# The head of a fused state-space and feed-forward kernel: tile 1 in two loads, weights ahead of tiles 2 and 3, all layernorm sums on VectorE, more of the first copies on ScalarE

## The chip, the cores and the metric

The kernel runs on one core of a Trainium2 chip. The metric is the device time of one execution in microseconds (us); lower is better. A profile records one execution; its span (first to last instruction) is mostly about 1.4 us shorter than the time that goes with it. All executions quoted here were in the fast state with a granted clock of 1.00.

## The reference

```python
xn = layernorm(x)                        # x: 2048 x 1024, bf16
A = 2 * real(C h) + xn * Dskip           # h[t] = Lam_bar * h[t-1] + B_bar xn[t], complex, 1024 states
B = (mish(x @ w1 + b1)) @ w2             # w1: 1024 x 3584, w2: 3584 x 1024, x here is xn
out = x + A + B
```

Both branches take the layernormed rows. They are worked in four blocks of 512 rows, each of four tiles of 128 rows. Everything that follows is about the first block's start, "the head": four tiles have to be loaded, normalised and transposed before the long run of matmuls can begin at full width.

## The kernel before

Each engine has its own program, a queue of operations in fixed order, with semaphore waits worked out from reads and writes. An operation that waits holds up all that stands behind it on its engine (in after_short below, VectorE stands 1.39 us at one tile's sums, and another tile's apply waits behind them). All loads of the head are issued by SyncE in this order: tile 0 in two halves, tile 1, tile 3, weight load 1, tile 2, weight loads 2 to 6, the skip weights, weight load 7. (The code's `ring` items are counted from 1 here; each is 512 KB.)

```python
    for h in range(2):
        SP.dma(lambda e, h=h: e.dma_start(xx[:, 0, 0, h * 512:(h + 1) * 512], A_x[0, 0:P, h * 512:(h + 1) * 512]),
               DmaSem(nc, "d_x00_%d" % h), writes=[b_xx[0][0].parts[h]])
    for q in (1, 3):
        load_x(SP, 0, q)
    # ... cut: small parameter loads ...
    for i in range(NRING):
        ring_load()
        if i == 0:
            load_x(SP, 0, 2)
        if i == 5:
            SP.dma(...)                      # skip weights, 256 KB
```

Tiles 0 to 2 get mean and variance on VectorE (`first_sums_v` twice, `first_var_v`), tile 3 gets them on ScalarE (two passes with accumulation). The root is taken on ScalarE; reciprocal and `first_apply` (subtract mean, multiply) are on VectorE. PE transposes the normalised tile, and `first_copy` brings it from PSUM to `xnT`. Fillers, matmuls on zeros, are meant to keep PE's clock up while it waits.

```python
    def keep_busy(n, behind=()):             # n fillers, all into PSUM bank 3
        for i in range(n):
            PE.mm(...)                       # 128 x 128; the first waits for `behind` and for bank 3

    keep_busy(36)
    for q in range(2):
        first_sums_v(q, 0); first_sums_v(q, 1); first_var_v(q); first_sqrt(q)
    keep_busy(14, [b_mv[0]])
    PE.op(...)                               # transpose of the parameters
    keep_busy(8, [b_mv[1]])
    first_apply(0)
    first_transpose(0)
    first_apply(1, 2)
    first_transpose(1)
    keep_busy(8)
    first_mean_a(3)                          # tile 3 on ScalarE
    first_copy(0, VE, 0, 4); first_copy(1, VE, 0, 4)
    first_copy(0, AC, 4, NK); first_copy(1, AC, 4, NK)
    first_center_a(3)
    # ... cut: parameters out of PSUM ...
    for h in range(2):
        first_sums_v(2, h)
    first_var_v(2)
    first_var_a(3)
    first_sqrt(2); first_sqrt(3)
    first_apply(2); first_apply(3)
    NSPLIT = 5
```

The first weight columns f are multiplied in two halves. The first half (tiles 0 and 1, 256 columns wide) can start while tiles 2 and 3 are still on their way; the second half follows in the main loop. Each `first_half(f, 0)` is eight matmuls over k. Weight loads 1 and 2 hold the lower and upper k of f = 0 to 3, loads 3 and 4 those of f = 4 to 7.

```python
    for f in range(4):
        first_half(f, 0, 0, NK // 2)         # load 1
    for f in range(4):
        first_half(f, 0, NK // 2, NK)        # load 2
        if f in (2, 3):
            first_transpose(f)
            first_copy(f, VE)
    first_half(4, 0)                         # loads 3 and 4
    # main loop: first_half(f, 1) for f < NSPLIT, then whole columns from f = NSPLIT on
```

Of the kernel before, what the change touches and what calls it, by code (L numbers as in the profile page):

```python
# [5 lines left out]
ALU = mybir.AluOpType  # L6
AF = mybir.ActivationFunctionType
DT = mybir.dt

P = 128  # L10
# [146 lines left out]
def build_kernel(nc, A_x, A_Lambda_re, A_Lambda_im, A_B_re, A_B_im, A_C_re, A_C_im,  # L157
                 A_log_dt, A_Dskip, B_w1, B_b1, B_w2, out):
    bf16, f32, i32 = DT.bfloat16, DT.float32, DT.int32
    S, D = A_x.shape[1], A_x.shape[2]  # L160
# [15 lines left out]
    VE = Queue(nc, "ve")  # L176
    AC = Queue(nc, "ac")
    PO = Queue(nc, "po")
    SP = Queue(nc, "sp")

    def sb(name, shape, dtype):
        return nc.alloc_sbuf_tensor(name, shape, dtype)
# [25 lines left out]
    xx = sb("xx", [P, 2, NQ, D], bf16)  # L208
    b_xx = [[Buf("xx%d_%d" % (i, q), parts=[Buf("xx%d_%d_%d" % (i, q, h)) for h in range(2)])
             for q in range(NQ)] for i in range(2)]  # L210
# [16 lines left out]
    mv = sb("mv", [P, NQ, 2], f32)  # L227
    b_mv = [Buf("mv%d" % i) for i in range(NQ)]
    rs = sb("rs", [P, NQ, 4], f32)
    b_rs, b_rs1 = ([Buf("rs%s%d" % (n, i)) for i in range(NQ)] for n in "ab")  # L230
    kon = sb("kon", [P, 3], f32)
    b_kon = Buf("kon")
# [9 lines left out]
    def c(n):  # L242
        return cs[:, CN.index(n), :]
# [7 lines left out]
    def ps16(i):  # L251
        return ps[:, i, :].bitcast(bf16)
# [6 lines left out]
    def scratch(name, where, i, dtype, n):  # L259
        if where == "h":  # L260
            t = nc.alloc_sbuf_tensor_at(name, [P, n], dtype, offset=base_h + 2048 * i)
            return t, Buf(name, parts=flat_hT[2 * i:2 * i + 2])
        t = nc.alloc_sbuf_tensor_at(name, [P, n], dtype, offset=base_a + 2048 * i)
        return t, Buf(name, parts=b_actf[2 * i:2 * i + 2])
# [11 lines left out]
    vop, aop, pop = VE.op, AC.op, PO.op  # L276
# [7 lines left out]
    def load_x(queue, blk, q):  # L284
        r0 = blk * TB + q * P
        i = blk % 2
        queue.dma(lambda e: e.dma_start(xx[:, i, q, :], A_x[0, r0:r0 + P, :]),  # L287
                  s_xx[i][q] if blk else s_x0[q], writes=[b_xx[i][q]])

    for h in range(2):  # L290
        SP.dma(lambda e, h=h: e.dma_start(xx[:, 0, 0, h * 512:(h + 1) * 512], A_x[0, 0:P, h * 512:(h + 1) * 512]),
               DmaSem(nc, "d_x00_%d" % h), writes=[b_xx[0][0].parts[h]])
    for q in (1, 3):
        load_x(SP, 0, q)
    for src, r0, n in ((A_log_dt, 2 * NJ, NJ), (A_Lambda_im, NJ, NJ), (A_Lambda_re, 0, NJ),
                       (B_b1, 3 * NJ, NF)):
        AC.dma(lambda e, src=src, r0=r0, n=n: e.dma_start(
# [24 lines left out]

    for i in range(NRING):
        ring_load()
        if i == 0:
            load_x(SP, 0, 2)
        if i == 5:
            SP.dma(lambda e: e.dma_start(dsk[:], A_Dskip.partition_broadcast(P)), s_dsk, writes=[b_dsk])

# [11 lines left out]



    sq, b_sq = scratch("sq", "a", 13, bf16, D)

    def rc(q, n):
        return rs[:, q, n:n + 1]

    def first_sums_v(q, h):
        s = q % 2  # L350
        vop(lambda e: e.bn_stats(stats[:, s, h, :], xx[:, 0, q, h * 512:(h + 1) * 512]),  # L351
            reads=[b_xx[0][q].parts[h]], writes=[b_stats[s]])

    def first_var_v(q):
        s = q % 2
        vop(lambda e: e.bn_aggr(mv[:, q, :], stats[:, s, :, :]), reads=[b_stats[s]], writes=[b_mv[q]])  # L356

    def first_mean_a(q):
        aop(lambda e: e.activation(sq[:], xx[:, 0, q, :], AF.Identity, bias=kon[:, 1:2], accum_out=rc(q, 3)),
            reads=[b_xx[0][q], b_kon], writes=[b_sq, b_rs[q]])  # L360

    def first_center_a(q):
        aop(lambda e: e.activation(mv[:, q, 0:1], rc(q, 3), AF.Copy, scale=-1.0 / D),
            reads=[b_rs[q]], writes=[b_mv[q]])

    def first_var_a(q):
        aop(lambda e: e.activation(sq[:], xx[:, 0, q, :], AF.Square, bias=mv[:, q, 0:1], accum_out=mv[:, q, 1:2]),
            reads=[b_xx[0][q], b_mv[q]], writes=[b_sq, b_mv[q]])

    def first_sqrt(q):  # L370
        scale = 1.0 if q < 3 else 1.0 / D
        aop(lambda e: e.activation(rc(q, 1), mv[:, q, 1:2], AF.Sqrt, scale=scale, bias=kon[:, 2:3]),
            reads=[b_mv[q], b_kon], writes=[b_rs1[q]])

    def first_apply(q, pieces=1):
        y = rc(q, 1)
        vop(lambda e: e.reciprocal(y, y), reads=[b_rs1[q]], writes=[b_rs1[q]])  # L377
        for h in range(pieces):
            d = slice(h * D // pieces, (h + 1) * D // pieces)
            b_x, b_o = (b_xx[0][q], b_xn[q]) if pieces == 1 else (b_xx[0][q].parts[h], b_xn[q].parts[h])  # L380
            vop(lambda e, d=d: e.tensor_scalar(xn[:, q, d], xx[:, 0, q, d], mv[:, q, 0:1], y,
                                               op0=ALU.subtract if q < 3 else ALU.add, op1=ALU.mult),
                reads=[b_x, b_mv[q], b_rs1[q]], writes=[b_o])

    def bank_T(q, k):
        if q < 2 and k >= NK // 2:
            return 4 + q
        return 6 + q % 2

    def first_transpose(q):  # L390
        for k in range(NK):
            bank = bank_T(q, k)
            PE.mm(lambda e, k=k, bank=bank: e.transpose(ps16(bank)[:, k * P:(k + 1) * P],  # L393
                                                        xn[:, q, k * P:(k + 1) * P], ident[:]),
                  reads=[b_xn[q].parts[k // (NK // 2)], b_ident], writes=[b_ps[bank]],
                  first=k == 0 or bank != bank_T(q, k - 1), last=k == NK - 1 or bank != bank_T(q, k + 1))

    def first_copy(q, queue, k0=0, k1=NK):
        dst = xnT[:, k0:k1, q * P:(q + 1) * P]
        bank = bank_T(q, k0)  # L400
        srcp = ps16(bank).rearrange("p (k t) -> p k t", k=NK)[:, k0:k1, :]
        b_dst = b_xnT[q] if k1 - k0 == NK else b_xnT[q].parts[k0 // 4]
        if queue is AC:
            aop(lambda e: e.copy(dst, srcp), reads=[b_ps[bank]], writes=[b_dst])
        else:
            vop(lambda e: e.tensor_copy(dst, srcp), reads=[b_ps[bank]], writes=[b_dst])
# [68 lines left out]
    def keep_busy(n, behind=()):  # L475
        for i in range(n):
            PE.mm(lambda e: e.matmul(ps[:, 3, 0:P], lhsT=filler[:], rhs=filler[:], start=True, stop=True),  # L477
                  reads=[b_filler] + (list(behind) if i == 0 else []), writes=[b_ps[3]], first=i == 0, last=i == n - 1)

    keep_busy(36)  # L480
    aop(lambda e: e.activation(rs[:, :, 3], kon[:, 2:3].to_broadcast([P, NQ]), AF.Sqrt), reads=[b_kon], writes=b_rs)
    for q in range(2):
        first_sums_v(q, 0)
        first_sums_v(q, 1)
        first_var_v(q)
        first_sqrt(q)
    keep_busy(14, [b_mv[0]])
    PE.op(lambda e: e.transpose(ps16(2)[:, 0:NST], st[:, :], ident[0:NST, 0:NST]),
          reads=[b_st, b_ident], writes=[b_ps[2]])
    keep_busy(8, [b_mv[1]])  # L490
    first_apply(0)
    first_transpose(0)
    first_apply(1, 2)
    first_transpose(1)
    keep_busy(8)
    first_mean_a(3)
    first_copy(0, VE, 0, 4)
    first_copy(1, VE, 0, 4)
    first_copy(0, AC, 4, NK)
    first_copy(1, AC, 4, NK)  # L500
    first_center_a(3)
    vop(lambda e: e.tensor_copy(par[:, :], ps16(2)[:, 0:NST]), reads=[b_ps[2]], writes=[b_par])
    for h in range(2):
        first_sums_v(2, h)
    first_var_v(2)
    first_var_a(3)
    first_sqrt(2)
    first_sqrt(3)
    first_apply(2)
    first_apply(3)  # L510
    NSPLIT = 5

    def w1_tile(base, f, k):

# [4 lines left out]
    def first_half(f, half, k0=0, k1=NK):  # L519
        ts = slice(half * 256, half * 256 + 256)  # L520
        for k in range(k0, k1):
            s, w = w1_tile(0, f, k)
            PE.mm(lambda e, k=k, w=w: e.matmul(ps[:, f, ts], lhsT=w, rhs=xnT[:, k, ts],  # L523
                                               start=k == 0, stop=k == NK - 1),
                  reads=[b_ring[s]] + [b.parts[k // 4] for b in b_xnT[2 * half:2 * half + 2]], writes=[b_ps[f]],
                  first=half == 0 and k == 0, last=half == 1 and k == NK - 1)
# [2 lines left out]
        first_half(f, 0, 0, NK // 2)  # L529
    for f in range(4):  # L530
        first_half(f, 0, NK // 2, NK)
        if f in (2, 3):
            first_transpose(f)
            first_copy(f, VE)
    first_half(4, 0)
    aop(lambda e: e.activation(c("dt"), ldt, AF.Exp), reads=[b_par], writes=[b_cs["dt"]])
    small("a", "dt", lre, ALU.mult)
    small("th", "dt", lim, ALU.mult)
# [120 lines left out]
    def first_tile(blk, f):  # L659
        bank, hs = f % 8, f % (2 * GF)  # L660
        if blk == 0 and f < NSPLIT:
            first_half(f, 1)
        for k in range(0 if blk == 0 and f < NSPLIT else NK):
            s, w = w1_tile(n_item[0], f % 4, k)
# [236 lines left out]
```

## Time and profile before

| | before |
|---|---|
| median time | 621.53 us (3 executions), 621.50 us (6) |
| span of the profile | 620.0 us |
| PE busy | 616.7 us, 99% |
| first real matmul | 8.70 us |
| second halves begin | 14.17 us |

The page of the kernel before: span, busy time by engine, the clock granted in 40 slices (tenths), and one of the costliest groups (busy us and mean ns, then idle time ahead of it).

```profile
span 620.0 us, 7386 instructions
...
PE 616.7 (99%) x2961; PEld 287.2 (46%) x2961; DVE 462.4 (75%) x677; ACT 247.6 (40%) x161; POOL 50.6 (8%) x47
...
PEclk9999999999999999999999999999999999999999
...
L665 PE MATMUL ps<-xnT,ring 128*128 128x512 bf16 x856 | 185.4, 379 | 0.0
```

PE is busy 99% of the time, and this group, like PE's other great ones, has 0.0 us of idle time ahead of it. Busy PE time is not a measure of how near PE is to its peak, but the missing waits say that only the head can be shortened by rearranging.

The timeline of PE's weight loads (PEld) of the kernel before shows the head's order. Its columns are start, length, engine, line, operation, output and inputs, forms, count, and in brackets the idle time before and what ended it. PEld is used because all weight loads have records, while some matmul records are missing in the traces (the changed kernel's page counts 2981 loads and 2925 matmuls). "xn" marks transposes, "xnT,ring" real matmuls.

```profile
7.13 1.07 PEld L393 LDWEIGHTS ps<-ident,xn 128*128 128x128 bf16 x16 [0.16 <-DVE xn L381]
8.16 0.49 PEld L477 LDWEIGHTS ps<-filler 128*128 128x128 bf16 x8
8.70 1.66 PEld L523 LDWEIGHTS ps<-xnT,ring 128*128 128x128 bf16 x16
10.57 1.21 PEld L523 LDWEIGHTS ps<-xnT,ring 128*128 128x128 bf16 x12 [0.21 <-DMA ring<-in_B_w_dram]
11.88 0.46 PEld L393 LDWEIGHTS ps<-ident,xn 128*128 128x128 bf16 x8
12.29 0.37 PEld L523 LDWEIGHTS ps<-xnT,ring 128*128 128x128 bf16 x4
12.67 0.54 PEld L393 LDWEIGHTS ps<-ident,xn 128*128 128x128 bf16 x8
13.17 0.81 PEld L523 LDWEIGHTS ps<-xnT,ring 128*128 128x128 bf16 x8
14.17 4.26 PEld L523 LDWEIGHTS ps<-xnT,ring 128*128 128x128 bf16 x40 [0.19 <-DVE xnT L406]
```

Fillers and the transposes' first wait (0.16 us) last until 7.13 us. Sixteen transposes and eight more fillers follow, and the first real matmul comes at 8.70. After it there are three holes worth naming: 0.21 us for weight load 2, 0.10 us ahead of tile 2's transposes (11.78 to 11.88), and 0.19 us for tile 3's copy. The second halves begin at 14.17.

The timeline of VectorE (DVE) of the kernel before, in the same columns:

```profile
9.05 1.42 DVE L351 BATCH_NORM_STATS2 stats<-xx 128x6 f32<-128x512 bf16 x2 [0.34 <-DMA xx<-in_A_x_dram]
...
11.28 0.55 DVE L381 TENSOR_SCALAR xn<-xx,mv,rs 128x1024 bf16<-128x1024 bf16 x1
11.74 0.16 DVE L377 RECIPROCAL rs<-rs 128x1 f32<-128x1 f32 x1
12.00 0.55 DVE L381 TENSOR_SCALAR xn<-xx,mv,rs 128x1024 bf16<-128x1024 bf16 x1
12.54 0.69 DVE L406 COPY xnT<-ps 128x1024 bf16<-128x1024 bf16 x1
13.43 0.69 DVE L406 COPY xnT<-ps 128x1024 bf16<-128x1024 bf16 x1 [0.19 <-PE ps L393]
```

VectorE waits 0.34 us for tile 2's load, then does tile 2's sums, and applies tile 2 (11.28) and tile 3 (12.00) one after the other. Nothing of tile 3's sums stands between them.

Landings are not in these lines. I read them from the trace as the end of a load's last transfer: in this profile tile 1 at 4.78 us, tile 3 at 5.92, weight load 1 at 7.59, tile 2 at 9.02, load 2 at 10.53, load 3 at 12.04, load 4 at 13.54.

### The profile page before, as it was taken

To read this page: it belongs to the slowest core of one execution; us is meant where nothing else is said; L and a number is where in the kernel's file an instruction comes from. 1 tells how busy PE (TensorE), PEld (TensorE's weight loads), DVE (VectorE), ACT (ScalarE), POOL (GpSimd) and SP (SyncE) were. 2 spreads that over 40 slices of the span, in tenths; PEclk is the share of its full clock that TensorE was granted. 3 is DMA by queue.
4 is the path that set the end of the run, shared out by engine and by line. 5 is a ranking of instruction groups with operands and counts; after the bars stand their busy time and mean duration, and the time that the engine had idled before them with its cause. 6 is when DMAs were issued, how large, how long until landed. Compare 5 with 4: busy or idle time off the path is not lost.

```text
span 620.0 us, 7386 instructions
## 1 busy us (share of the span) xinstructions
PE 616.7 (99%) x2961; PEld 287.2 (46%) x2961; DVE 462.4 (75%) x677; ACT 247.6 (40%) x161; POOL 50.6 (8%) x47
## 2 busy tenths in 40 slices
PE   9999999999999999999999999999999999999998
PEld 7544444444444444444444444444444444444444
DVE  7897999999467599998147659999624856999603
ACT  5689996440079940000008992000001999000000
POOL 1998000000100000000010000000000000000000
PEclk9999999999999999999999999999999999999999
DMA  8999956840364301783054430276203542033001
GB/s 282 255 294 248 220 111 190 218 136 0 124 204 147 135 1 36 205 197 107 17 187 135 150 122 1 85 204 174 82 35 104 169 167 69 1 122 117 1 0 69
DMA packets 95804, 79.41 MB, mean 128 GB/s; under 512 B 48922, under 2 KB 78234, under 8 KB 95770
## 3 DMA queue, kind: packets, MB, share of 16 engines
q1 hardware_dynamic: 92272, 71.64, 42.1%
q10 hardware_dynamic: 2538, 4.14, 1.8%
q0 software_dynamic: 960, 3.15, 1.6%
q8 instruction: 24, 0.39, 0.3%
q14 instruction: 10, 0.08, 0.0%
HBM read 63.19 MB, written 4.19 MB: 109 GB/s over the span
## 4 chain that ended last, share of the span: by engine, by line
PE 99%; DVE 1%; DMA 0%; issue 0%; DVEq 0%
PE ps L744 49%; PE ps L665 30%; PE ps L686 18%; PE ps L523 1%; DVE stats L351 0%; DMA xx<-in_A_x_dram 0%; PE ps L393 0%; PE ps L758 0%; PE ps L477 0%; DVE xx L812 0%; DVE mv L356 0%; DVE rs L377 0%; DVEq L131 0%
## 5 line engine op out<-in xcount | busy, mean ns | idle before, releaser
L744 PE MATMUL ps<-ring,act 128*128 128x512 bf16 x896 | 194.0, 379 | 0.0
L665 PE MATMUL ps<-xnT,ring 128*128 128x512 bf16 x856 | 185.4, 379 | 0.0
L644 ACT ACTIVATE act<-hb 128x3584 bf16<-128x3584 bf16 x16 | 50.9, 3183 | 224.1 <-DVE hb L673 224.0
L744 PEld LDWEIGHTS ps<-ring,act 128*128 128x128 bf16 x896 | 87.7, 98 | 105.7
L665 PEld LDWEIGHTS ps<-xnT,ring 128*128 128x128 bf16 x856 | 83.7, 98 | 100.8
L673 DVE TENSOR_SCALAR hb<-ps,par 128x512 bf16<-128x512 f32 x112 | 82.4, 747 | 56.0 <-PE ps L665 54.8
L686 PE MATMUL ps<-xnT,BT 128*128 128x512 bf16 x512 | 111.2, 379 | 0.0
L744 PE MATMUL ps<-CT,hT 128*128 128x512 bf16 x506 | 109.9, 379 | 0.0
L691 DVE TENSOR_TENSOR mt<-ps,tab 128x1024 bf16<-128x1024 f32 x64 | 75.4, 1219 | 17.5 <-PE ps L686 16.6
L686 PEld LDWEIGHTS ps<-xnT,BT 128*128 128x128 bf16 x512 | 50.1, 98 | 60.4
L744 PEld LDWEIGHTS ps<-CT,hT 128*128 128x128 bf16 x506 | 49.5, 98 | 59.7
L709 DVE TENSOR_TENSOR_SCAN hT<-cs,qi,hT 128x512 bf16<-128x512 f32 x48 | 58.9, 1269 | 0.0
L789 DVE TENSOR_TENSOR xx<-ps,xx 128x1024 bf16<-128x1024 f32 (+1 forms) x16 | 18.8, 1190 | 46.0 <-PE ps L744 45.9
L645 ACT ACTIVATE act<-act 128x3584 bf16<-128x3584 bf16 x16 | 51.0, 3190 | 0.2
L646 ACT ACTIVATE act<-act 128x3584 bf16<-128x3584 bf16 x16 | 51.0, 3190 | 0.2
L714 DVE TENSOR_TENSOR mt<-hT,tab 128x1024 bf16<-128x1024 bf16 x64 | 41.4, 688 | 1.1
L651 DVE TENSOR_TENSOR act<-act,hb 128x3584 bf16<-128x3584 bf16 x16 | 32.3, 2017 | 1.3 <-ACT act L646 1.3
L287 POOL DMA_DIRECT2D xx<-in_A_x_dram x12 | 6.7, 559 | 253.2 <-DVE xx L789 247.9
L620 ACT ACTIVATE ct<-CT,cs 128x512 f32<-128x512 bf16 x16 | 11.5, 720 | 26.7 <-DVE CT L622 25.9
L645 ACT ACT_TABLE_LOAD x16 | 20.5, 1283 | 0.3
L646 ACT ACT_TABLE_LOAD x16 | 20.5, 1283 | 0.3
L709 DVE TENSOR_TENSOR_SCAN hT<-cs,hT 128x512 bf16<-128x512 f32 x16 | 18.7, 1209 | 0.0
(86 smaller groups left out, 276.7 us busy)
## 6 DMA issues: line engine op xcount, KB each, us to landing
ring<-in_B_w_dram SPq DMA_DIRECT2D x112, 512.0 KB, 4.1
out_dram<-xx ACTq DMA_DIRECT2D x15, 256.0 KB, 2.1
xx<-in_A_x_dram POOLq DMA_DIRECT2D x12, 256.0 KB, 3.5
xx<-in_A_x_dram SPq DMA_DIRECT2D x3, 256.0 KB, 3.7
xx<-in_A_x_dram SPq DMA_DIRECT2D x2, 128.0 KB, 2.2
dsk<-in_A_Dskip_dram SPq DMA_DIRECT2D x1, 256.0 KB, 8.2
xnT<-xn SPq DMA_TRANSPOSE x12, 4.6
BT<-in_A_B_re_dram SPq DMA_TRANSPOSE x8, 6.2
```

The costliest lines, as they stand in the source:

```text
L644: aop(lambda e: e.activation(a, hs, AF.Exp), reads=[b_hb[g % 2]], writes=[b_act[g]])
L645: aop(lambda e: e.activation(a, a, AF.Ln, bias=1.0), reads=[b_act[g]], writes=[b_act[g]])
L646: aop(lambda e: e.activation(a, a, AF.Tanh), reads=[b_act[g]], writes=[b_act[g]])
L651: vop(lambda e: e.tensor_tensor(a, a, hs, op=ALU.mult), reads=[b_act[g], b_hb[g % 2]], writes=[b_act[g]])
L665: PE.mm(lambda e, k=k, w=w: e.matmul(ps[:, bank, :], lhsT=w, rhs=xnT[:, k, :], start=k == 0, stop=k == NK - 1), reads=[b_ring[s]] + b_xnT, ...
L673: vop(lambda e: e.tensor_scalar(hb[:, hs, :], ps[:, bank, :], b1(f), None, op0=ALU.add), reads=[b_ps[bank], b_par], writes=[b_hbf[hs]])
L686: PE.mm(lambda e, j=j, ci=ci, k=k, bank=bank: e.matmul(ps[:, bank + ci, :], lhsT=BT[:, ci, j, k, :], rhs=xnT[:, k, :], start=k == 0, stop= ...
L691: vop(lambda e, s=s, u=u, j=j: e.tensor_tensor(mt[:, s, :, :], u, tab[:, s, j, :].unsqueeze(1).to_broadcast([P, 2, TB]), op=ALU.mult), rea ...
L709: vop(lambda e, ci=ci, init=init: e.tensor_tensor_scan(out=hT[:, ci, j, :], data0=cj("r", j).to_broadcast([P, TB]), data1=hT[:, ci, j, :], ...
L714: vop(lambda e, s=s: e.tensor_tensor(mt[:, s, :, :], hT[:, :, j, :], tab[:, s, j, :].unsqueeze(1).to_broadcast([P, 2, TB]), op=ALU.mult), ...
L744: PE.mm(lambda e: e.matmul(ps[:, u, :], lhsT=lhsT, rhs=rhs, start=st_, stop=last), reads=reads, writes=[b_ps[u]], first=st_, last=last)
L789: vop(lambda e: e.tensor_tensor(xr, src, xr, op=ALU.add), reads=b_ps[bank:bank + n] + [b_x], writes=[b_x])
```

## The change

The intent is to have weights earlier, to get rid of ScalarE's two passes over tile 3, and to use ScalarE for copies instead. The price is that tile 3 arrives later. A sixth column's first half gives PE work meanwhile, and the filler counts are set anew.

```diff
-    for h in range(2): ...                  # tile 0 in two halves
-    for q in (1, 3):
-        load_x(SP, 0, q)
+    for q in range(2):
+        for h in range(2): ...              # tiles 0 and 1 in two halves each
@@
-        if i == 0:
-            load_x(SP, 0, 2)
+        if i < 2:
+            load_x(SP, 0, 2 + i)            # tile 2 behind weight load 1, tile 3 behind load 2
@@
-    keep_busy(36)
+    keep_busy(40)
@@
-    keep_busy(14, [b_mv[0]])
+    keep_busy(20, [b_mv[0]])
@@
-    keep_busy(8, [b_mv[1]])
+    keep_busy(10, [b_mv[1]])
@@
-    first_mean_a(3)
-    first_copy(0, VE, 0, 4)
+    first_copy(0, AC, 0, 4)
@@
-    first_center_a(3)
@@
-    first_var_a(3)
     first_sqrt(2)
+    first_sums_v(3, 0)
+    first_apply(2)
+    first_sums_v(3, 1)
+    first_var_v(3)
     first_sqrt(3)
-    first_apply(2)
     first_apply(3)
-    NSPLIT = 5
+    NSPLIT = 6
@@
-        if f in (2, 3):
-            first_transpose(f)
-            first_copy(f, VE)
+        if f == 2:
+            first_transpose(2)
+            first_copy(2, AC)
     first_half(4, 0)
+    first_transpose(3)
+    first_copy(3, VE)
+    first_half(5, 0)
```

One detail that the argument comes to rest on: `first_half(4, 0)`, which needs weight loads 3 and 4, used to stand behind tile 3's transposes and now stands ahead of them.

More of the change, by code (lines that the diff above doesn't have):

```diff
@@ L288, in load_x @@
                   s_xx[i][q] if blk else s_x0[q], writes=[b_xx[i][q]])
-    for h in range(2):
-        SP.dma(lambda e, h=h: e.dma_start(xx[:, 0, 0, h * 512:(h + 1) * 512], A_x[0, 0:P, h * 512:(h + 1) * 512]),
-               DmaSem(nc, "d_x00_%d" % h), writes=[b_xx[0][0].parts[h]])
-    for q in (1, 3):
-        load_x(SP, 0, q)
+    for q in range(2):
+        for h in range(2):
+            SP.dma(lambda e, q=q, h=h: e.dma_start(xx[:, 0, q, h * 512:(h + 1) * 512],
+                                                   A_x[0, q * P:(q + 1) * P, h * 512:(h + 1) * 512]),
+                   DmaSem(nc, "d_x0%d_%d" % (q, h)), writes=[b_xx[0][q].parts[h]])
     for src, r0, n in ((A_log_dt, 2 * NJ, NJ), (A_Lambda_im, NJ, NJ), (A_Lambda_re, 0, NJ),
@@ L340, in build_kernel @@
     pop(lambda e: e.tensor_copy(iot[:], iot_i[:]), reads=[b_iot_i], writes=[b_iot])
-    sq, b_sq = scratch("sq", "a", 13, bf16, D)
     def rc(q, n):
@@ L356, in first_var_v @@
         vop(lambda e: e.bn_aggr(mv[:, q, :], stats[:, s, :, :]), reads=[b_stats[s]], writes=[b_mv[q]])
-    def first_mean_a(q):
-        aop(lambda e: e.activation(sq[:], xx[:, 0, q, :], AF.Identity, bias=kon[:, 1:2], accum_out=rc(q, 3)),
-            reads=[b_xx[0][q], b_kon], writes=[b_sq, b_rs[q]])
-    def first_center_a(q):
-        aop(lambda e: e.activation(mv[:, q, 0:1], rc(q, 3), AF.Copy, scale=-1.0 / D),
-            reads=[b_rs[q]], writes=[b_mv[q]])
-    def first_var_a(q):
-        aop(lambda e: e.activation(sq[:], xx[:, 0, q, :], AF.Square, bias=mv[:, q, 0:1], accum_out=mv[:, q, 1:2]),
-            reads=[b_xx[0][q], b_mv[q]], writes=[b_sq, b_mv[q]])
     def first_sqrt(q):
-        scale = 1.0 if q < 3 else 1.0 / D
-        aop(lambda e: e.activation(rc(q, 1), mv[:, q, 1:2], AF.Sqrt, scale=scale, bias=kon[:, 2:3]),
+        aop(lambda e: e.activation(rc(q, 1), mv[:, q, 1:2], AF.Sqrt, bias=kon[:, 2:3]),
             reads=[b_mv[q], b_kon], writes=[b_rs1[q]])
@@ L381, in first_apply @@
             vop(lambda e, d=d: e.tensor_scalar(xn[:, q, d], xx[:, 0, q, d], mv[:, q, 0:1], y,
-                                               op0=ALU.subtract if q < 3 else ALU.add, op1=ALU.mult),
+                                               op0=ALU.subtract, op1=ALU.mult),
                 reads=[b_x, b_mv[q], b_rs1[q]], writes=[b_o])
```

## The prediction

> **What bounds it now.** The matrix engine (PE): the page gives 616.7 us busy in a span of 620.0 us (99%), granted clock 1.00, and the chain of waits is 99% PE from 6.5 us on. After 18.4 us PE waits for nothing (idle before its groups: 0.0). So only the head can move the time. In the timeline the head is: fillers to 7.0 us, 16 transposes from 7.13, eight fillers, first real matmul at 8.70; then small holes (0.21 us for weight load 2 at 10.57, 0.10 for the transposes of tile 2 at 11.88, 0.19 for tile 3's copy at 14.17). Second-half matmuls start at 14.17. All together are about 0.55 us: the change can hardly gain or lose more than 1 us.
>
> **What the change does, costed from the trace.**
> 1. Weights ahead of tiles 2 and 3. Landings now: tile 1 4.8 us, tile 3 5.9, weight load 1 7.6, tile 2 9.1, weight load 2 10.5: about cumulative bytes (the Trainium skill, "DMA: Bandwidth & Descriptors", Queues, rings and completion order: descriptors are consumed in ring order). Expected after: load 1 about 6.6, tile 2 about 8.1, load 2 about 9.5, tile 3 about 10.6. The 0.21 us hole goes.
> 2. Tile 1 in two loads: its sums start at most 0.1 us earlier.
> 3. Tile 0's first copy moves from VectorE (0.42 us) to ScalarE (0.56 us), in parallel with tile 1's. Worth up to 0.3 us, if nothing else gates the first matmul.
> 4. But fillers do gate: 40+20+10 instead of 36+14+8. Each group starts only once the last one has drained (4.75 us last start, 5.18 next start). PE clock: pitch 107 ns until 5.6 us, 56 ns after. Four more at 107 ns, six and two at 56 ns put the transposes at about 7.6 instead of 7.13, and the first real matmul at about 9.0 instead of 8.70: +0.3 us.
> 5. Tile 3's sums move to VectorE, in series (1.42 us plus 0.21). One half stands before tile 2's apply. Tile 2's apply then ends at about 12.1 (now 11.82), and behind it come half of the sums 0.72, aggregate 0.21, root 0.3, reciprocal and apply 0.75, transposes, copy 0.69: tile 3's columns are ready at about 15.6. Now they are ready at 14.12.
> 6. To cover this, a sixth first half goes ahead: 8 matmuls, 0.87 us, so the corresponding point of before is 15.04. Net +0.55 us of PE holes.
> 7. The exponential behind tile 2's copy on ScalarE comes 2 to 3 us later, and so do the first bias evictions (15.5 to about 17.5). PE needs the first bank back only at about 23: free.
>
> **Prediction.** 622.0 us, that is +0.5; range 621.2 to 622.6. Faster by over 2%: 0.01; within 2%: 0.98; slower by over 2%: 0.01. Chance that it is slower at all: about 75%.
>
> **What would show it.** First real matmul at 8.9 to 9.1 us; weight load 2 landing before it is wanted; waits of PE for tile 2's and tile 3's normalised rows of 0.1 to 0.4 us each; second-half matmuls beginning at about 15.5 (break even is 15.04); no PE hole after 25 us.
>
> **What would make it wrong.** If the clock rises earlier, the extra fillers cost nothing and steps 1 and 3 gain 0.3 us. If tile 3 lands by 10 us, the VectorE chain shortens by half a microsecond and the result is even. If the clock rises a window later, the fillers at 107 ns cost a further 0.5 us.

## The result

| | before | after |
|---|---|---|
| median, lowest, highest (6 executions each) | 621.50, 621.30, 621.96 us | 621.86, 621.25, 622.01 us |
| span of the profile | 620.0 us | 619.8 us |
| first real matmul in the profile | 8.70 us | 8.52 us |
| second halves begin in the profile | 14.17 us | 14.87 us, with 8 more matmuls done |

The ratio of the fast runs is 1.0003, with a 95% interval of 0.9991 to 1.0016: the same at the 2% that counts. Ratios here are the mean time of one kernel's fast runs over that of the other's of the same rounds, so not quite the ratio of the medians that are quoted. The profile is of the fastest of the six executions (621.25 us), so it does not show what the other five paid for.

The page of the changed kernel:

```profile
span 619.8 us, 7370 instructions
...
PE 613.6 (99%) x2925; PEld 288.3 (47%) x2981; DVE 463.1 (75%) x678; ACT 246.6 (40%) x158; POOL 50.4 (8%) x47
```

The timeline of PE's weight loads of the changed kernel:

```profile
7.02 1.07 PEld L379 LDWEIGHTS ps<-ident,xn 128*128 128x128 bf16 x16
...
8.52 2.96 PEld L509 LDWEIGHTS ps<-xnT,ring 128*128 128x128 bf16 x28
11.49 0.54 PEld L379 LDWEIGHTS ps<-ident,xn 128*128 128x128 bf16 x8
11.99 0.81 PEld L509 LDWEIGHTS ps<-xnT,ring 128*128 128x128 bf16 x8
12.96 0.33 PEld L509 LDWEIGHTS ps<-xnT,ring 128*128 128x128 bf16 x4 [0.16 <-DMA ring<-in_B_w_dram]
13.30 0.54 PEld L379 LDWEIGHTS ps<-ident,xn 128*128 128x128 bf16 x8
13.80 0.81 PEld L509 LDWEIGHTS ps<-xnT,ring 128*128 128x128 bf16 x8
14.87 5.15 PEld L509 LDWEIGHTS ps<-xnT,ring 128*128 128x128 bf16 x48 [0.25 <-issue]
```

The first real matmul came at 8.52 us, 0.18 earlier than before and not 0.3 later. The hole for weight load 2 has gone, but a new one of 0.16 us for weight load 4, in front of the last four matmuls of column 4, which now stand ahead of tile 3's transposes. I put the last hole, 0.25 us ahead of the second halves, down to tile 3's copy, which ends at 14.75; the label "issue" means only that the releaser was not recognised. (In every profile of the changed kernel and its variants but all_three the second halves begin 0.12 us after this copy ends.)

The timeline of VectorE of the changed kernel:

```profile
10.01 0.64 DVE L350 BATCH_NORM_STATS2 stats<-xx 128x6 f32<-128x512 bf16 x1
10.56 0.15 DVE L363 RECIPROCAL rs<-rs 128x1 f32<-128x1 f32 x1
10.75 0.55 DVE L367 TENSOR_SCALAR xn<-xx,mv,rs 128x1024 bf16<-128x1024 bf16 x1
11.21 0.69 DVE L350 BATCH_NORM_STATS2 stats<-xx 128x6 f32<-128x512 bf16 x1
...
12.70 0.55 DVE L367 TENSOR_SCALAR xn<-xx,mv,rs 128x1024 bf16<-128x1024 bf16 x1
14.06 0.69 DVE L392 COPY xnT<-ps 128x1024 bf16<-128x1024 bf16 x1 [0.81 <-PE ps L379]
```

Half of tile 3's sums stands ahead of tile 2's apply, and the other half behind it, as the diff says. Tile 3's copy waits 0.81 us for PE's transposes, not the other way round: VectorE is not late here.

To compare the two heads I add 0.87 us (eight matmuls at 109 ns) to the kernel before's begin of second halves. The changed kernel's 14.87 then answers to 15.05 (these sums are taken before rounding). From that point to the end the spans agree: 604.95 to 604.98 us in all of the profiles of both kernels and of the variants below, but for one with 605.06. So nothing behind the head matters, and every further question is about the begin of the second halves. "Begin" means that point below.

### The profile page after: what moved, and what is told of

The parts are those of the page before. It is cut to its first block, busy times and chain, and to the rows that moved or that the text cites. A ratio compares the mean times of both kernels' runs of the same rounds, so it can differ in the third digit from the quotient of the medians.

```text
span 619.8 us, 7370 instructions
## 1 busy us (share of the span) xinstructions
PE 613.6 (99%) x2925; PEld 288.3 (47%) x2981; DVE 463.1 (75%) x678; ACT 246.6 (40%) x158; POOL 50.4 (8%) x47
## 4 chain that ended last, share of the span: by engine, by line
PE 95%; ACT 2%; DVE 2%; issue 1%; DVEq 0%
PE ps L733 49%; PE ps L654 26%; PE ps L675 18%; PE ps L463 1%; PE ps L509 1%; ACT act L635 1%; ACT act L634 1%; ACT act L633 1%; DVE hb L662 0%; DVE stats L350 0%; DVE act L640 0%; PE ps L747 0%; ACT L634 0%; ACT L525 0%; ACT xnT L390 0%
## 5 line engine op out<-in xcount | busy, mean ns | idle before, releaser
L654 PE MATMUL ps<-xnT,ring 128*128 128x512 bf16 x832 | 182.7, 379 | 0.8
L634 ACT ACT_TABLE_LOAD x16 | 20.5, 1283 | 0.3
L635 ACT ACT_TABLE_LOAD x16 | 20.5, 1283 | 0.3
```

The lines of the kernel that those rows point to most:

```text
L634: aop(lambda e: e.activation(a, a, AF.Ln, bias=1.0), reads=[b_act[g]], writes=[b_act[g]])
L635: aop(lambda e: e.activation(a, a, AF.Tanh), reads=[b_act[g]], writes=[b_act[g]])
L654: PE.mm(lambda e, k=k, w=w: e.matmul(ps[:, bank, :], lhsT=w, rhs=xnT[:, k, :], start=k == 0, stop=k == NK - 1), reads=[b_ring[s]] + b_xnT, ...
```

## The experiments

All variants gave correct results. Twelve kernels ran, in three calls of four; those of a call share a chip and the runs of the kernel before. "Before, same call" is 621.30 us (11 executions) in the first, 621.63 (9) in the second and 621.20 (9) in the third. The 95% intervals reach about 0.0012, or 0.75 us, to either side, so that medians which differ by a few tenths of a microsecond do not settle anything by themselves, least of all across calls. What the argument rests on is the profiles.

### First call: is it the fillers?

The PE clock shows in the fillers' pitch, 107 ns at first and 56 ns later. The Trainium skill, "TensorE: Matmul & The Clock Gate", Part 1, gives 106.7 and 55.6 ns for 128 columns in its two clock states, and says that the change between them is run-variable. The trace agrees: in the profile of before the pitch falls at 5.6 us, in that of after at 4.09. Theory A was therefore that the changed kernel is slow when the clock rises late, because it then spends longer on its added fillers. The rival, theory B, was late loads and the VectorE chain behind them.

**after_again**: the changed kernel, no edit.

> The changed kernel, unaltered, for a second profile and more times. In its first profile the PE clock rose at 4.09 us (filler pitch 107 to 56 ns), in that of the kernel before at 5.6. Theory A (the clock's moment decides): two clusters of times, about 621.3 when it rises near 4 us and 621.8 to 622.0 when it rises near 5.6; whatever this profile shows, span and rise must agree: rise near 4.1 gives first real matmul at 8.5 and a span of 619.8; rise near 5.6 gives transposes at 7.5 to 7.6, first matmul near 9.0, span 620.3 to 620.6. Theory B (the serial VectorE chain or late loads): the spread comes with other landings of tile 3, first matmul at 8.5 always.

Measured: 622.08 us median of 5 (621.49 to 622.38); ratio to before 1.0009 (0.9997 to 1.0021). The profile has its clock rise at 4.11 us, first matmul at 8.54, begin at 15.10, span 620.1. The rise is as early as in the first profile, yet the begin is 0.23 us later. That goes with weight load 4, which landed at 13.16 instead of 12.92:

```profile
13.20 0.33 PEld L509 LDWEIGHTS ps<-xnT,ring 128*128 128x128 bf16 x4 [0.37 <-DMA ring<-in_B_w_dram]
...
15.10 5.15 PEld L509 LDWEIGHTS ps<-xnT,ring 128*128 128x128 bf16 x48 [0.25 <-ACT cs L525]
```

This too is the profile of the fastest execution of its run. The two profiles do not show theory A's late case.

**before_again**: the kernel before, no edit.

> The kernel before against itself: ratio 1.000 within 0.0005, and a second profile. Theory A: if the clock rises near 5.6 us again, first real matmul at 8.70 as before; if near 4.1, nearly the same (8.55 to 8.70), because the shorter fillers are done in time either way; times 621.3 to 621.6 with few exceptions. Theory B says nothing of the clock.

Measured: 621.52 us median of 5 (621.01 to 622.23); ratio to the same kernel 1.0003 (0.9991 to 1.0015). This is the noise. The clock rose at about 6.1 us, the first matmul came at 8.85, the begin at 14.20, span 620.0. Loads 2 and 4 landed at 9.90 and 12.91 and were not waited for. So with a late rise the first matmul came 0.15 us later than in the first profile of before, and the begin only 0.03.

**after_short**:

```diff
-    keep_busy(40)
+    keep_busy(36)
-    keep_busy(20, [b_mv[0]])
+    keep_busy(14, [b_mv[0]])
-    keep_busy(10, [b_mv[1]])
+    keep_busy(8, [b_mv[1]])
```

> The changed kernel with the filler counts of the kernel before (36, 14, 8 in place of 40, 20, 10), nothing else. Theory A: the slow cluster goes; first matmul at 8.5 to 8.7 at either clock moment, times 621.1 to 621.5, median about 0.4 below the changed kernel and 0.1 to 0.2 below the kernel before. Theory B: no difference from the changed kernel (621.86) beyond 0.1.

Measured: 622.27 us median of 6 (621.57 to 623.98); ratio 1.0015 (1.0003 to 1.0027). The fillers of before do not bring the time of before back; theory A is not borne out as the main cause. The profile, of an execution of 623.18 us, shows what does cost. PE's weight loads in it:

```profile
8.51 1.66 PEld L509 LDWEIGHTS ps<-xnT,ring 128*128 128x128 bf16 x16
10.78 1.21 PEld L509 LDWEIGHTS ps<-xnT,ring 128*128 128x128 bf16 x12 [0.60 <-DMA ring<-in_B_w_dram]
12.87 0.45 PEld L379 LDWEIGHTS ps<-ident,xn 128*128 128x128 bf16 x8 [0.89 <-DVE xn L367]
...
14.47 0.33 PEld L509 LDWEIGHTS ps<-xnT,ring 128*128 128x128 bf16 x4 [0.39 <-DMA ring<-in_B_w_dram]
...
16.38 5.15 PEld L509 LDWEIGHTS ps<-xnT,ring 128*128 128x128 bf16 x48 [0.25 <-issue]
```

The first matmul is on time (8.51). Then PE waits 0.60 us for weight load 2, 0.89 us for tile 2's normalised rows and 0.39 us for load 4. Tile 2 itself had landed at 7.70 us. Its apply waited because VectorE stood 1.39 us at tile 3's first sums, for a tile that landed at 11.45 us (9.91 in the first profile of after, 5.92 in that of before).

**before_long**: the opposite edit, the kernel before with 40, 20 and 10.

> The kernel before with the filler counts of the changed one (40, 20, 10), nothing else. Theory A: two clusters, the kernel before's 621.4 when the clock rises near 4 us and 621.8 to 622.0 when near 5.6; median 0.3 to 0.5 above the kernel before. Theory B: as the kernel before, within 0.1.

Measured: 621.46 us median of 5 (621.09 to 621.95); ratio 1.0001 (0.9989 to 1.0012). In the times the fillers cost nothing that can be told from noise. In the profile, of the slowest of the five, they do: clock rise at 6.3 us, first matmul at 9.35, begin at 14.71, that is 0.51 us later than in before_again with nearly the same rise. So the mechanism of theory A is real, but it is no more than one part.

### Second call: is it weight load 4, or tile 3?

In three profiles of the changed kernel and its short-filler variant the begin came 1.94 to 1.95 us after load 4's landing. Behind that landing stand, in series, four matmuls, tile 3's transposes, the eight matmuls of column 5 and the rest of the copy's time. I called this theory C. Theory B was narrowed to tile 3's landing in front of tile 2's apply.

**load4_last**:

```diff
-    first_half(4, 0)
+    first_half(4, 0, 0, NK // 2)
+    first_half(5, 0, 0, NK // 2)
     first_transpose(3)
     first_copy(3, VE)
-    first_half(5, 0)
+    first_half(4, 0, NK // 2, NK)
+    first_half(5, 0, NK // 2, NK)
```

> The changed kernel with PE's order alone altered: what needs weight load 4 (second k halves of weight columns 4 and 5) stands behind tile 3's transposes instead of the fifth column ahead of them. Theory C (weight load 4 sets the head of the changed kernel): in the three profiles of the changed kernel and its short-filler variant, second-half matmuls began 1.94 us after load 4 landed (landing 12.92, 13.16, 14.43; begin 14.87, 15.10, 16.38). With the order altered the serial part behind the landing is about 0.9 us, so the begin should be at about 14.8 for any landing up to 13.8: span 619.7 to 619.9, median time 621.0 to 621.4, slow end of the spread below 622. Theory B (tile 3's landing in front of tile 2's apply): the spread stays as it was, 621.3 to 622.4, median near 621.9.

Measured: 621.98 us median of 5 (621.84 to 622.26); ratio 1.0006 (0.9994 to 1.0019). Theory C alone had foreseen 621.0 to 621.4: a miss. The median is 0.35 us above before in the same call. The changed kernel itself was not in this call (in the other two it lay 0.78 and 0.99 us above before), so it is not shown whether the edit gained anything against it. PE's weight loads in its profile:

```profile
12.11 0.45 PEld L379 LDWEIGHTS ps<-ident,xn 128*128 128x128 bf16 x8 [0.51 <-DVE xn L367]
...
14.06 0.45 PEld L379 LDWEIGHTS ps<-ident,xn 128*128 128x128 bf16 x8 [0.30 <-DVE xn L367]
...
15.53 5.15 PEld L509 LDWEIGHTS ps<-xnT,ring 128*128 128x128 bf16 x48 [0.25 <-issue]
```

Load 4 (13.71) is no longer waited for. Both transposes now wait for their normalised rows, 0.51 and 0.30 us: tile 3 landed at 10.70, and VectorE waited 0.48 us for it ahead of tile 2's apply. Begin at 15.53, which is 4.83 us after tile 3's landing.

**x3_ahead**:

```diff
-        if i < 2:
-            load_x(SP, 0, 2 + i)
+        if i < 1:
+            load_x(SP, 0, 2)
+            load_x(SP, 0, 3)
```

> The changed kernel with tile 3's load issued ahead of weight load 2 instead of behind it; bytes ahead of load 4 unchanged. Theory B: tile 3 lands near 8.5 to 9 us, VectorE never waits for it, the slow end goes: median 621.3. Theory C: no gain; load 4 lands when it did, second halves begin 1.94 us later: median 621.7 to 622.1; load 2 lands near 10 and gives a hole of 0 to 0.3 us that only moves the later one.

Measured: 621.96 us median of 5 (621.56 to 622.38); ratio 1.0005 (0.9993 to 1.0018). Theory B alone had foreseen 621.3: a miss. The median is 0.33 us above before in the same call, and again it is not shown whether that is a gain against the changed kernel. In its profile tile 3 landed at 8.85 and nothing waited for it. The clock, however, was first seen up at 7.1 us, so that the first matmul came at 9.70 and the begin, 6.29 us later, at 15.99. This is theory A's case, in which neither tile 3 nor load 4 has a say.

**dsk_early_after**: the load of the skip weights, 256 KB, just ahead of weight load 4.

```diff
-        if i == 5:
+        if i == 2:
             SP.dma(...)                      # skip weights
```

> The changed kernel with the load of the skip weights (256 KB) pulled from behind weight load 6 to just ahead of weight load 4, so load 4 lands about 0.7 us later, tile 3 as before. Theory C: the whole of it shows, +0.6 to +0.8 us against the changed kernel: median about 622.6, begin of second halves again 1.94 us after load 4. Theory B: no change (tile 3's load is ahead of it).

Measured: 622.85 us median of 5 (622.34 to 623.36); ratio 1.0021 (1.0008 to 1.0035). That is 0.9 us above the two variants of the changed kernel in the same call (621.98 and 621.96); the changed kernel itself was not in this call. PE's weight loads in its profile:

```profile
14.42 0.33 PEld L509 LDWEIGHTS ps<-xnT,ring 128*128 128x128 bf16 x4 [0.69 <-DMA ring<-in_B_w_dram]
...
16.33 5.15 PEld L509 LDWEIGHTS ps<-xnT,ring 128*128 128x128 bf16 x48 [0.25 <-issue]
```

Load 4 landed at 14.38 and was waited for 0.69 us. The begin at 16.33 is again 1.95 us later. The lateness of load 4 passes to the end one for one once it is waited for.

**dsk_early_before**: the same edit in the kernel before.

> The kernel before with the same shift of the skip weights. Theory C: there only 0.5 us of work stand between load 4 and the second halves, and load 4 lands 0 to 0.6 us ahead of need, so only part shows: +0.2 to +0.5 us, median about 621.7. Theory B: none.

Measured: 622.01 us median of 5 (621.48 to 623.12); ratio 1.0009 (0.9997 to 1.0022), so 0.4 us above before in the medians. In its profile load 4 landed at 13.77:

```profile
13.81 4.70 PEld L523 LDWEIGHTS ps<-xnT,ring 128*128 128x128 bf16 x44 [0.20 <-DMA ring<-in_B_w_dram]
```

PE waited 0.20 us for it. The second halves began at 14.23, only 0.46 us later; with the 0.87 us that make the two heads comparable this is 1.33 against the changed kernel's 1.95.

### Third call: all at once

Theory D was that the begin is the latest of several ends, so that one cure only uncovers the next. The variants combine the short fillers, x3_ahead and load4_last; the edits are those shown.

**all_three**: short fillers, x3_ahead and load4_last.

> The changed kernel with all three: the shorter fillers of the kernel before, tile 3's load ahead of weight load 2, and what needs weight load 4 behind tile 3's transposes. Theory D (the begin of the second halves is the latest of three ends: first matmul + 6.2 us, weight load 4's landing + 1.95, tile 3's landing + 4.8; so single cures do nothing): all three are now relaxed, the begin is near 14.8 to 15.0 in nearly every run (15.05 is where it equals the kernel before): median 0.1 to 0.3 us below the kernel before and 0.6 below the changed kernel. If D is wrong and something else in the changed head costs the time, it stays with the changed kernel near 621.9.

Measured: 621.68 us median of 5 (621.14 to 623.36); ratio 1.0011 (0.9999 to 1.0024). It is 0.51 us below the changed kernel in the same call, as expected, but 0.48 above before, which was not. Two executions (621.14, 621.33) are at before's level by their times.

Here the spans say more than the times. In three of the five executions (623.36, 622.31, 621.68) the time is 1.86 to 1.91 us longer than the span; in two of after_short and one of x3_and_short it is 1.78 to 1.93, in all other executions whose spans are on record 1.35 to 1.47. Why is not known, but the extra 0.4 us lies outside the span, and so outside the head. The five spans are 621.5, 619.7, 620.4, 619.9 and 619.8: the median, 619.9, is 0.1 us above before's in the same call (619.8) and 0.9 below the changed kernel's (620.8). So by the spans theory D's forecast, a begin at 14.8 to 15.0, came true in two of the five (span less 604.98) and a begin at 14.7 in a third.

The profile is of the slowest, 623.36 us:

```profile
11.14 1.21 PEld L510 LDWEIGHTS ps<-xnT,ring 128*128 128x128 bf16 x12 [0.70 <-DMA ring<-in_B_w_dram]
...
15.70 6.01 PEld L510 LDWEIGHTS ps<-xnT,ring 128*128 128x128 bf16 x56 [1.04 <-DMA ring<-in_B_w_dram]
```

Here load 2 landed at 11.10 and load 4 at 15.66, later than in any other profile (10.73 and 14.43 are the next). The altered order on PE did not cover that: the second halves began at 16.48.

**x3_and_load4**: without the short fillers.

> The same without the shorter fillers. Theory D: as all_three when the clock rises early; when it rises at 6 us or later, first matmul at 9.3 to 9.7 and begin of second halves at 15.5 to 16.0. Median between all_three and the changed kernel, spread wider than all_three's.

Measured: 621.64 us median of 5 (621.45 to 622.37); ratio 1.0008 (0.9995 to 1.0020). As all_three, 0.55 us below the changed kernel. Its spread was narrower, not wider. By the spans it is 620.2 against 620.8 and before's 619.8. In the profile load 2 landed at 10.48 and was waited for 0.39 us; begin at 15.05:

```profile
10.52 1.21 PEld L510 LDWEIGHTS ps<-xnT,ring 128*128 128x128 bf16 x12 [0.39 <-DMA ring<-in_B_w_dram]
...
15.05 5.15 PEld L510 LDWEIGHTS ps<-xnT,ring 128*128 128x128 bf16 x48 [0.21 <-ACT cs L528]
```

**x3_and_short**: without the altered PE order.

> The same without the altered PE order. Theory D: begin of the second halves is weight load 4's landing (12.9 to 14.4) + 1.95, so 14.9 to 16.3: median near the changed kernel's, 0.2 to 0.6 us above all_three.

Measured: 622.12 us median of 5 (621.70 to 622.53); ratio 1.0014 (1.0001 to 1.0026). As the changed kernel. Load 4 landed at 13.44, begin at 15.39: 1.95 us.

**after_third**: the changed kernel, no edit.

> The changed kernel once more, as a control on the same chip: 0.3 to 0.6 us above the kernel before, median 621.8 to 622.1. In its profile the begin of the second halves is the latest of first matmul + 6.2, load 4 + 1.95, tile 3 + 4.8, within 0.1 us.

Measured: 622.19 us median of 5 (622.02 to 622.92); ratio 1.0017 (1.0003 to 1.0030). This profile has the late clock that the first two lacked:

```profile
5.61 1.40 PEld L463 LDWEIGHTS ps<-filler 128*128 128x128 bf16 x20 [0.39 <-DVE stats L350]
...
7.83 0.94 PEld L379 LDWEIGHTS ps<-ident,xn 128*128 128x128 bf16 x16
...
9.30 2.97 PEld L509 LDWEIGHTS ps<-xnT,ring 128*128 128x128 bf16 x28
...
14.05 0.33 PEld L509 LDWEIGHTS ps<-xnT,ring 128*128 128x128 bf16 x4 [0.47 <-DMA ring<-in_B_w_dram]
...
15.96 5.15 PEld L509 LDWEIGHTS ps<-xnT,ring 128*128 128x128 bf16 x48 [0.25 <-ACT cs L525]
```

The fillers' second group starts at 5.61, the transposes at 7.83, the first real matmul at 9.30: 0.3 us later than I had predicted for a rise at 5.6, and the rise was at 6.2. Then load 4, landed at 14.01, is waited for 0.47 us, and the begin is at 15.96.

### The four ends side by side

For the changed kernel: the first matmul + 6.23 us (PE without a wait for a load; 0.19 us of waiting for tile 3's copy are in it), load 2 + 4.53, tile 3 + 4.83, load 4 + 1.95. The constants are read from profiles in which that end was last: before_again (6.23), before (load 2), load4_last (tile 3) and after (load 4). The begin should be the latest. For the kernel before (0.87 us added) the constants are 6.23, 4.52 and, for load 4, 1.33 (from dsk_early_before); tile 3 has landed by 5.9 us there.

| profile | first matmul + 6.23 | load 2 + 4.5 | tile 3 + 4.83 | load 4 + 1.95 (before: + 1.33) | begin measured |
|---|---|---|---|---|---|
| after | 14.75 | 13.74 | 14.74 | **14.87** | 14.87 |
| after_again | 14.77 | 14.00 | 14.97 | **15.11** | 15.10 |
| after_third | 15.53 | 14.39 | 15.37 | **15.96** | 15.96 |
| after_short | 14.74 | 15.26 | 16.28 | **16.38** | 16.38 |
| dsk_early_after | 15.67 | 14.07 | 15.08 | **16.33** | 16.33 |
| x3_and_short | 14.70 | 14.94 | 13.73 | **15.39** | 15.39 |
| x3_ahead | **15.93** | 14.88 | 13.68 | 15.31 | 15.99 |
| before (+ 0.87) | 14.93 | **15.05** | – | 14.87 | 15.05 |
| before_again (+ 0.87) | **15.08** | 14.42 | – | 14.24 | 15.08 |
| before_long (+ 0.87) | **15.58** | 14.78 | – | 14.59 | 15.58 |
| dsk_early_before (+ 0.87) | **15.11** | 14.37 | – | 15.10 | 15.11 |

A constant read from a profile fits that profile of necessity; the other rows are the test, and the latest of the four is within 0.06 us of the begin in each. Those rows test load 4's end and the first matmul's; load 2's and tile 3's were last in no row of the changed kernel. The three variants with an altered PE order are left out, as less work stands behind load 4 there: 0.82 us in all_three (15.66 to 16.48). With that, x3_and_load4 should begin at load 2 + 4.53 = 15.01, and it began at 15.05.

## Why the prediction was right or wrong

The time was right: 622.0 predicted, 621.86 measured over 6 executions, and 622.08 and 622.19 in two more calls of 5. The sign, slower by a little, held in the medians of all three calls (+0.36, +0.78, +0.99 us), though the interval of the ratio excludes 1 only in the last. The reasons were partly wrong, and the right number owes something to luck: it was made of late fillers (+0.3 us) and of waits for tiles 2 and 3, and in two of the three profiles neither came, while waits for load 4, which the prediction does not have, came in all three.

**Only the head can matter: right.** The rest of the span was 604.95 to 604.98 us in all profiles but one, whatever the head did. The later bias evictions (16.40 instead of 15.50 us in the first profiles) cost nothing.

**Step 1, weights earlier: half right.** Load 1 was expected at 6.6 us and landed at 7.08, 6.88 and 7.67 in the three profiles of the changed kernel (7.59 and 7.04 before): no clear gain. Load 2 came at 9.21, 9.47 and 9.86 (9.5 expected), and its hole did go in those. Tile 3 came at 9.91, 10.14 and 10.54 (10.6 expected).

**Step 2, tile 1 in two loads: right in size.** VectorE began tile 1's sums at 4.67 instead of 4.80 us.

**Step 4, the fillers: mis-sized, and at most a part of the cause.** The term was +0.3 us at the first matmul. It was 8.52 and 8.54 (–0.18) with a clock rise near 4.1 us, and 9.30 (+0.6) with a rise at 6.2. Taking the added fillers away gained nothing in the median, and giving them to the kernel before cost nothing there. The profiles do show a cost when the clock rises late: with 40, 20 and 10 fillers the first real matmul came at 9.30 to 9.70 us in four of eight profiles, with 36, 14 and 8 it came at 8.88 at the latest in six. In after_third the late first matmul alone would have put the begin at 15.53, 0.45 us behind before_again's. That the prediction named both ways in which the clock could make it wrong does not save the term.

**Step 5, the VectorE chain: right as a path, wrong as the usual limit.** Tile 3's columns were expected at 15.6 us and were ready at 14.75 in the first profile, although the copy had waited 0.81 us for PE. The waits of PE for the normalised rows of tiles 2 and 3, 0.1 to 0.4 us each in the prediction, are in none of the three profiles of the changed kernel (the longest hole there is 0.06 us); in their place PE waited 0.16, 0.37 and 0.47 us for load 4. In load4_last the VectorE chain was last; in after_short it came within 0.1 us.

**The step that was missing: what stands behind weight load 4.** I took the net loss as the VectorE chain minus the 0.87 us of a sixth column, and did not see that column 4's matmuls had moved ahead of tile 3's transposes. In the changed kernel 1.95 us of work stand behind load 4's landing, in the kernel before 1.33 on the same scale. In all three of its profiles load 4 is the last of the four ends, with begins of 14.87, 15.10 and 15.96 against before's 15.05 and 15.08. Delaying load 4 delayed the begin one for one (dsk_early_after). Relaxing load 4 and tile 3 together gave back 0.51 and 0.55 us in the medians of the same call (all_three, x3_and_load4), 0.9 and 0.6 us by the spans; tile 3 with the fillers gave 0.07 (x3_and_short). The intervals of these runs overlap, and for load4_last and x3_ahead there is no changed kernel in the call to compare with. So where a profile shows lost time at load 4, it is because the changed head asks for later loads, sooner, with more work in series behind them. That this also makes the loss in the medians is argued and not shown: landings are known for one execution of each run, and of the changed kernel's three profiles only after_third's shows a loss against before. There the begin is 0.88 us behind before_again's, 0.45 of it from the late first matmul and 0.43 from load 4 (with before's 1.33 the same landing would give 15.34, short of the 15.53 of the first matmul). The gain that the change looked for, weight load 2 in time and a first matmul 0.18 us earlier, is there in two of its three profiles; waits for weight load 4 took 0.16 and 0.37 us of it back.

**What stays open.** Why all_three and x3_and_load4 still lie 0.4 to 0.5 us above before in the same call. For all_three the longer part outside the span makes most of it in the median (by the spans it is 0.1 us). Load 2 stands behind tile 3 in both; it landed at 11.10 and 10.48 in their two profiles and was waited for, which would do it, but two profiles do not settle it. Why one load lands up to 1.5 us later in one execution than in the next is not known either. Nor is it tested whether the new order itself makes load 4 land later: with nothing added ahead of it, it landed at 12.91 to 13.54 us in three profiles of the kernel before and its variants, and at 12.92 to 15.66 (median 13.71) in nine of the changed kernel and its variants. No version that beats both kernels was found.

## What to carry to other kernels

In a head that several loads and engines feed, write down for each load how much serial work stands behind its landing, and compare these sums before and after a change of order: a load that just arrives in time can cost what its sum grows by. When one cure brings less than expected, look whether another end lies just under the first, and take several away together. When the profile is the fastest of its executions, take more profiles before explaining a median by it. And keep an unedited control in every call: without it, a variant's median cannot be set against the change.

## What the Trainium skill lacked or had wrong

- "TensorE: Matmul & The Clock Gate", Part 1, What's actually happening: it says that the moment of the clock's rise varies by ±500 ns, with the phase of a free-running window. In these 14 profiles, with the first filler always at 1.03 to 1.04 us, the faster pitch was first seen between 4.09 and 7.09 us, a range of 3 us. Fillers have to be counted for the late case too. The two pitches (106.7 and 55.6 ns) and 109 ns for 256 columns agree with the page.
- "DMA: Bandwidth & Descriptors", Queues, rings and completion order: it says that completion is not first in, first out for one issuing engine, and it gives no spread. Here SyncE's loads landed in the order of their issue in all 14 profiles, so that no run shows the page's case. The same weight load 4, with the same bytes ahead of it, landed between 12.91 and 15.66 us in the 12 profiles in which it was not delayed on purpose. A head that is tuned to one profile's landings is tuned to one execution.
- "ScalarE: Activation LUTs", What ACT_TABLE_LOAD costs: 1283 ns for the load agrees with every one here. The 1380 ns of DRAIN that the page adds does not show: in the profile of before ScalarE's work ended at 11.23 us, the load ran from 11.25 to 12.53, and the next ACTIVATE began at 12.54.
- No page that I found has a duration for the layernorm sums on VectorE. Here 128 x 512 elements in bf16 took 0.64 to 0.70 us, and the aggregate 0.21 us.
